# A two-layer decode kernel on one core: K in four interleaved DMAs for each pair of batches, `wo` in 4 KB runs, the stashed V returned later, and rstd applied after the projections

## The chip, the cores and the metric

The kernel runs on one core of one Trainium2 chip. The metric is device time in microseconds (us) of one execution. Ten of the 11 runs of before beside e5 lie within 0.5% of their median (185.98 us; 185.21 to 187.26). The profile is taken of one execution; its span, from the first to the last record, is some 2 us shorter than the device time.

## The reference

Four residual steps for 4 sequences of one token each: attention over a cache, a gated feed-forward block, and both again with the same weights. All arrays are bf16, D = 512, 32 query heads, 8 key heads, head size 128, F = 1792. The last W = 2048 positions of an 8192-long cache are used.

```python
def A(x, k_cache, v_cache, wq, wo):            # cut to what matters
    q = heads(x @ wq)                          # [4, 32, 1, 128]
    k = repeat(k_cache[:, :, Sk - W:, :], 4)   # W = 2048
    v = repeat(v_cache[:, :, Sk - W:, :], 4)
    p = softmax(q @ k.T * 128 ** -0.5)
    return merge(p @ v) @ wo

def B(x, w_gate, w_up, w_down):
    return (sigmoid(x @ w_gate) * (x @ w_up)) @ w_down

x = x + A(layernorm(x)); x = x + B(layernorm(x))
x = x + A(layernorm(x)); x = x + B(layernorm(x))
```

## The kernel before

K (16.8 MB) is loaded once and stays in SBUF for both attentions. V, `wq` and the feed-forward weights are streamed twice through a pool of 1 MB slots, `wo` is loaded once and kept. All DMAs but the 4 KB of x are issued by SyncE on one queue, in program order; each waits until a slot is free. A key head's 4 batches are two "pairs" of 1 MB: partition 2r + b holds row r (of 64) of batch b of the pair, and a row is 32 keys, 8 KB in one run.

```python
def pair_d(cache, h, bp):      # 64 rows x 2 batches, runs of 8 KB
    return cache[2 * bp:2 * bp + 2, h, SK - W:SK, :].rearrange("b (p j) d -> p b (j d)", p=64)

def load_k(h):
    where[("K", h)] = h
    for bp in range(2):
        dma("K%d_%d" % (h, bp), kpair(h, bp), pair_d(A_k, h, bp), w=tok(4 * h + 2 * bp), rate="bw_8k")

wo_d = A_wo.rearrange("(q p) n -> p q n", p=128)      # runs of 1 KB
def load_wo(hh):
    load(("wo", hh), 4, "bw_1k", (2 * SLOT, wo_d[:, hh * 2 * REP:(hh + 1) * 2 * REP, :], False))
```

One V pair survives the first attention as a "stash": VectorE transposes it into four PSUM banks and later back into a slot (the "unstash", line L502 of the kernel before).

```python
STASH = SB + PBS
def load_stash(name):
    ...
    def emit(s):
        for n, b in enumerate(STASH):
            dst = tile_ap(s)[:, n * 1024:(n + 1) * 1024].bitcast(F32)
            o = P.op("vector", "us%d" % n, c_dve(512), lambda v, dst=dst, b=b: v.transpose(dst, ps[:, b, :]), ...)
            ...
# order of loads after the first feed-forward weights:
load_wq(1)
load_stash(("V",) + keep[0] + (1,))
for h in range(HKV)[::-1]:
    ...
            if (h, bp) not in keep:
                load_v(h, bp, 1, 1)
```

The layer norm computes mean, variance and rstd before it writes the normalised `xn`. The query of a head is expanded to a block form by four copies on VectorE and ScalarE.

```python
def layer_norm(tag, b0, b1):
    # x*x; both sums; one f32 matmul with ones; mean; mean^2; var; Ln; Exp(-0.5 .); x - mean; times rstd -> xn
    ...
def q_unit(tag, h, k2):
    for a in range(4):
        dst = qbd[32 * a:32 * a + 32, ...]; src = qrep[32 * a:32 * a + 32, ...]
        ...                                           # VectorE for even a, ScalarE for odd a
```

The score matmuls read K after a transposition in place, so neighbouring keys of one batch lie two and two; per head there are 32 + 32 matmuls on V and 16 on `wo`.

```python
kt = kpair(hk, b // 2).rearrange("p (j c x i t) -> p c t i j x", c=2, x=16, i=2, t=2)
last = pe.matmul(ps[32 * gi:32 * gi + NR, bank, :], qbd[:, q0:q0 + NR],
                 kt[:, cp // 2, cp % 2, b % 2, :, :], start=(cp == 0), stop=(cp == 3))
```

## Time and profile before

| | before |
|---|---|
| device time, median of 3 runs | 186.11 us (185.71 to 186.42) |
| span of the profiled run | 184.4 us |
| DMA queue 1: bytes, share of 16 engines' span | 71.84 MB, 97.2% |
| first attention ends / second attention's first score matmul | 108.0 / 129.2 us |
| last V or `wo` matmul of the second attention | 172.3 us |
| last feed-forward activation `hT` written / last `w_down` landed | 179.5 / 181.75 us |

From the page of the kernel before: the span; the packets by size; the queue's bytes and its share of the 16 DMA engines' time; the chain of waits by engine.

```profile
span 184.4 us, 4421 instructions
...
DMA packets 15379, 72.12 MB, mean 391 GB/s; under 512 B 1144, under 2 KB 5248, under 8 KB 8704
...
q1 hardware_dynamic: 15352, 71.84, 97.2%
...
DMA 52%; PE 25%; SPq 16%; DVE 4%; issue 2%; ACT 0%
```

The engines have a packet in flight nearly all the time, so the time is near the sum of all packets' durations. That sum, over 16 engines, is 180.6 us by the packet records; an 8 KB packet takes 311 ns (median), 4 KB 159 ns, 2 KB 84 ns, 1 KB 48 ns, a semaphore write 9 ns.

The windows view of the kernel before. The columns are the stretch and its length, busy us (and instructions) of each engine, the granted TensorE clock as a share of full speed, the busy share of the DMA engines, and GB/s. Where the trace holds no record of the clock, the view prints 1.00; in before that is so until 24.6 us.

```profile
13.00:21.00 8.00, 1.86 (x44) 0.68 (x48) 6.87 (x11) 1.71 (x6) 0.00 (x0) 1.00 1.01 427
120.00:124.00 4.00, 1.73 (x20) 0.76 (x17) 1.25 (x8) 0.41 (x2) 0.00 (x0) 0.50 0.96 344
124.00:128.00 4.00, 1.43 (x28) 0.34 (x24) 3.14 (x6) 0.00 (x0) 0.00 (x0) 0.50 1.03 417
128.00:132.00 4.00, 3.97 (x52) 1.20 (x44) 1.90 (x7) 1.82 (x7) 0.00 (x0) 0.70 1.08 351
132.00:136.00 4.00, 3.50 (x50) 1.03 (x40) 3.08 (x12) 2.11 (x6) 0.76 (x4) 1.00 0.94 350
```

The first row is the K stream at 427 GB/s. I put the two rows at 350 GB/s down to V reloads that are issued late, since the first slot that comes free goes to the unstash.

The end of before in the timeline (start, length, engine, line, operation; in brackets the idle time before it and what ended it):

```profile
179.29 0.22 DVE L874 TENSOR_TENSOR hT<-ebuf,eg 128x56 bf16<-128x56 f32 x1
...
179.93 1.04 PE L905 MATMUL ps<-arena,hT 128*4 128x256 bf16 x16 [1.09 <-DMA arena<-in_B_w_down_dram]
...
181.17 1.01 PE L905 MATMUL ps<-arena,hT 128*4 128x256 bf16 x12 [0.20 <-DMA arena<-in_B_w_down_dram]
```

The last matmuls wait for the last weights. But `hT`, which PE's chain delivers, was ready at 179.5 us, only 0.4 us before the first of these weights (179.89 us).

### The profile page before, as it was taken

The page shows a single profiled execution, that of the slowest core. Times are in us where ns is not written, and L with a number is a line of the kernel's source. Part 1 is how long each engine was busy: PE and PEld are TensorE (multiplying, and loading weights), DVE is VectorE, ACT ScalarE, POOL GpSimd, SP SyncE. Part 2 cuts the span into 40 slices and gives each one's busy share as a digit, 9 for nine tenths or more (in the row PEclk, how much of TensorE's full clock was granted, in tenths as well). Part 3 has the DMA queues.
Part 4 walks back from the last instruction along what each step waited for, and adds up shares of the span by engine and source line. Part 5 has one row for each costly group of instructions (what it writes and reads, how often), then busy time and mean ns, then how long its engine had stood idle before and what let it go on. Part 6 is the DMA issues. An engine that isn't in the chain of part 4 may idle for free.

```text
span 184.4 us, 4421 instructions
## 1 busy us (share of the span) xinstructions
PE 101.2 (55%) x1944; PEld 54.7 (30%) x1944; DVE 89.5 (49%) x221; ACT 35.7 (19%) x100; POOL 14.8 (8%) x77
## 2 busy tenths in 40 slices
PE   0532423652807327173373545445979997994474
PEld 0101000332303323023232441210334653584422
DVE  5209998477592565925621531138463442340330
ACT  2003022240212103011020001001365442220010
POOL 4000000110000101010010000000022111120000
PEclk9999995585766756755555555555897897885569
DMA  5999999999999999999999999999999999999980
GB/s 198 425 427 427 425 403 391 411 421 419 409 387 425 419 421 403 392 419 419 400 391 414 412 407 393 403 350 417 330 396 419 419 423 416 418 416 402 412 341 24
DMA packets 15379, 72.12 MB, mean 391 GB/s; under 512 B 1144, under 2 KB 5248, under 8 KB 8704
## 3 DMA queue, kind: packets, MB, share of 16 engines
q1 hardware_dynamic: 15352, 71.84, 97.2%
q8 instruction: 15, 0.25, 0.5%
q14 instruction: 4, 0.03, 0.0%
q10 hardware_dynamic: 8, 0.00, 0.0%
HBM read 71.83 MB, written 0.00 MB: 390 GB/s over the span
## 4 chain that ended last, share of the span: by engine, by line
DMA 52%; PE 25%; SPq 16%; DVE 4%; issue 2%; ACT 0%
DMA arena<-in_A_v_cache_dram 33%; SPq L382 16%; PE ps L697 11%; DMA arena<-in_B_w_down_dram 9%; PE ps L770 8%; DMA arena<-in_A_wq_dram 5%; DMA arena<-in_B_w_up_dram 5%; PE ps L726 2%; PE ps L794 1%; DVE ps L492 1%; PE ps L626 1%; DVE nmax L705 1%; PE ps L749 1%; PE ps L905 1%; PE ps L852 1%
## 5 line engine op out<-in xcount | busy, mean ns | idle before, releaser
L770 PE MATMUL ps<-ebuf,arena 128*128 128x8 bf16 x1024 | 31.0, 167 | 29.7 <-DMA arena<-in_A_v_cache_dram 22.1
L697 PE MATMUL ps<-arena,qbd 128*16 128x512 bf16 x256 | 32.5, 626 | 16.9 <-DVE qbd L668 8.4
L770 PEld LDWEIGHTS ps<-ebuf,arena 128*128 128x128 bf16 x1024 | 28.8, 101 | 36.3 <-DMA arena<-in_A_v_cache_dram 32.5
L678 DVE STREAM_TRANSPOSE arena<-arena 128x1024 f32<-128x1024 f32 x32 | 37.9, 1219 | 3.3 <-DMA arena<-in_A_k_cache_dram 3.0
L705 DVE TENSOR_REDUCE nmax<-ps 128x1 f32<-128x512 f32 x16 | 11.0, 687 | 26.0 <-PE ps L697 26.0
L714 ACT ACTIVATE prow<-ps,nmax 128x512 bf16<-128x512 f32 x16 | 11.0, 687 | 39.6 <-DVE nmax L711 24.9
L671 ACT COPY qbd<-qrep 32x64 bf16<-32x64 bf16 x32 | 7.7, 241 | 40.9 <-PE ps L697 40.3
L697 PEld LDWEIGHTS ps<-arena,qbd 128*16 128x16 bf16 x256 | 6.1, 97 | 31.3 <-issue 22.0
L739 POOL CAST s<-psm 128x1 bf16<-128x1 f32 x16 | 3.0, 188 | 144.4 <-ACT prow L714 144.4
L778 DVE TENSOR_TENSOR onb<-ps,rinv 128x16 bf16<-128x16 f32 x16 | 2.9, 184 | 21.1 <-PE ps L770 21.1
L626 PE MATMUL ps<-arena,xn 128*4 128x512 bf16 x64 | 7.8, 582 | 7.6 <-DMA arena<-in_A_wq_dram 6.2
L794 PE MATMUL ps<-onb,arena 128*128 128x4 bf16 x256 | 9.1, 166 | 3.1 <-DVE onb L778 3.1
L731 ACT CAST prow<-ps 128x512 bf16<-128x512 f32 x16 | 9.4, 587 | 7.1 <-PE ps L726 7.0
L735 DVE STREAM_TRANSPOSE ebuf<-prow 128x256 f32<-128x256 f32 x16 | 7.0, 437 | 6.7 <-ACT prow L731 6.4
L852 PE MATMUL ps<-arena,xn 128*4 128x448 bf16 x64 | 6.5, 560 | 4.9 <-DVE xn L607 3.1
L794 PEld LDWEIGHTS ps<-onb,arena 128*128 128x128 bf16 x256 | 7.9, 101 | 4.1 <-DVE onb L778 2.8
L726 PE MATMUL ps<-prow,perm 64*128 64x256 bf16 x64 | 7.4, 315 | 2.4 <-ACT prow L714 2.3
L596 ACT ACTIVATE lnv<-lnv 128x4 f32<-128x4 f32 x4 | 0.8, 205 | 34.0 <-DVE lnv L593 34.0
L634 DVE STREAM_TRANSPOSE ebuf<-ps 128x512 f32<-128x512 f32 x4 | 2.9, 715 | 7.7 <-PE ps L626 7.6
L859 DVE STREAM_TRANSPOSE ebuf<-ps 128x448 f32<-128x448 f32 x4 | 2.6, 650 | 7.8 <-PE ps L852 7.8
L668 DVE COPY qbd<-qrep 32x64 bf16<-32x64 bf16 x32 | 5.3, 166 | 0.7 <-ACT qrep L657 0.2
L749 PE MATMUL ps<-sel_b,s 128*128 128x16 bf16 x48 | 3.8, 175 | 3.2 <-POOL s L743 2.4
(61 smaller groups left out, 68.1 us busy)
## 6 DMA issues: line engine op xcount, KB each, us to landing
arena<-in_A_v_cache_dram SPq DMA_DIRECT2D x30, 1024.0 KB, 16.8
arena<-in_A_k_cache_dram SPq DMA_DIRECT2D x16, 1024.0 KB, 16.0
arena<-in_A_wq_dram SPq DMA_DIRECT2D x8, 1024.0 KB, 9.4
arena<-in_A_wo_dram SPq DMA_DIRECT2D x4, 1024.0 KB, 24.3
arena<-in_B_w_gate_dram SPq DMA_DIRECT2D x4, 896.0 KB, 19.7
arena<-in_B_w_up_dram SPq DMA_DIRECT2D x4, 896.0 KB, 15.8
arena<-in_B_w_down_dram SPq DMA_DIRECT2D x2, 1024.0 KB, 12.5
arena<-in_B_w_down_dram SPq DMA_DIRECT2D x1, 768.0 KB, 7.0
```

Of the source, the lines that this page charges most:

```text
L382: o = P.op("sync", name, 0.0, lambda e, dst=dst, src=src: e.dma_start(dst, src), r=r, w=w, dma_bytes=nbytes, dma_rate=tm[rate])
L626: last = pe.matmul(ps[32 * hh:32 * hh + NB, qb, :], xn[:, c * NB:(c + 1) * NB], tile_ap(s)[:, o + hh * 512:o + (hh + 1) * 512], start=(c = ...
L671: P.op("scalar", "qe%s_%d" % (tag, a), c_act(64), lambda s_, dst=dst, src=src: s_.copy(dst, src), r=rd, w=[("q", k2, a)])
L678: P.op("vector", "T%d_%d" % (h, t), c_dve(1024), lambda v, v32=v32: v.transpose(v32, v32), r=[("slot", 4 * h + t)], w=[("slot", 4 * h + t)])
L697: last = pe.matmul(ps[32 * gi:32 * gi + NR, bank, :], qbd[:, q0:q0 + NR], kt[:, cp // 2, cp % 2, b % 2, :, :], start=(cp == 0), stop=(cp = ...
L705: lambda v: v.tensor_reduce(nmax[:, k2:k2 + 1], ps[:, bank, :], AXX, ALU.max),
L714: lambda a: a.activation(prow[:, :].rearrange("p (m x t) -> p m x t", x=16, t=2), ps[:, bank, :].rearrange("p (m t x) -> p m x t", x=16, t ...
L726: last = pe.matmul(ps[:, PBS[i], 0:256], perm[64 * i:64 * i + 64, jh * 128:(jh + 1) * 128], prow[64 * i:64 * i + 64, jh * 256:(jh + 1) * 2 ...
L731: lambda a: a.copy(prow[:, :].rearrange("p (y i t) -> p i y t", i=2, t=2), ps[:, PBS[0]:PBS[0] + 2, 0:256].rearrange("p i (y t) -> p i y t ...
L770: last = pe.matmul(ps[:, ob, bp * 8:bp * 8 + 8], src[:, j * 128:(j + 1) * 128], ev[:, j % 2, j % 16 // 2, x0:x0 + 8], start=(j == 0), stop ...
L794: last = pe.matmul(ps[:, WB, c * NB:(c + 1) * NB], tile_ap(s)[:, o + r_ * D + c * 128:o + r_ * D + (c + 1) * 128], ov[:, r_ * NB:(r_ + 1) ...
L852: last = pe.matmul(ps[32 * g:32 * g + NB, OBS[n], 0:NF], xn[:, c * NB:(c + 1) * NB], tile_ap(s)[:, o:o + NF], start=(c == 0), stop=(c == N ...
```

## The change

The intent has four parts. (1) `wo` comes in runs of 4 KB; for that, the rows of o must be permuted, by four more matmuls and one masked VectorE product for each head. (2) Four neighbouring keys of a batch shall lie side by side after the transposition, so that the score matmuls read longer runs: partition 8y + 4b + x holds key block 4y + x of batch b. Where one DMA wrote a pair, four DMAs now write 32 partitions each, every fourth partition. (3) The stashed V comes back behind two V reloads; with that, its four transpositions change their order, and the first scores of the second attention go to another PSUM bank, which VectorE clears first. (4) rstd no longer stands before `xn`: it multiplies the gate and q afterwards, q is expanded by matmuls, and the sigmoid ends in a reciprocal on VectorE.

```diff
-    wo_d = A_wo.rearrange("(q p) n -> p q n", p=128)
+    wo_d = A_wo.rearrange("(h p m) n -> p h (m n)", p=128, m=REP)
 ...
         def load_k(h):
             for bp in range(2):
-                dma("K%d_%d" % (h, bp), kpair(h, bp), pair_d(A_k, h, bp), w=tok(4 * h + 2 * bp), rate="bw_8k")
+                src = A_k[2 * bp:2 * bp + 2, h, SK - W:SK, :].rearrange("b (y x j) d -> x y b (j d)", y=16, x=4)
+                for x in range(4):
+                    dma("K%d_%d%d" % (h, bp, x), kpair(h, bp)[x:128:4], src[x], w=[("k", 4 * h + 2 * bp, x)], rate="bw_8k")
 ...
-                        kt = kpair(hk, b // 2).rearrange("p (j c x i t) -> p c t i j x", c=2, x=16, i=2, t=2)
+                        kt = kpair(hk, b // 2).rearrange("p (j c y i x t) -> p c t i j y x", c=2, y=4, i=2, x=4, t=2)
 ...
+                    last = pe.matmul(ps[:, ob, 144 + m * NR:144 + (m + 1) * NR], permo[:, m * 128:(m + 1) * 128], ov,
+                                     start=True, stop=True)          # 4 for each head, then a masked product
 ...
-        load_stash(("V",) + keep[0] + (1,))
+                    n_v += 1
+                    if n_v == 2:
+                        load_stash(("V",) + keep[0] + (1,))
 ...
     # layer norm: xn = x - mean at once; variance() is called after the first projection's matmuls
+                    P.op("vector", "gs%d" % k, c_dve(NH),
+                         lambda v: v.tensor_tensor(egv, tv, lnr[:, 0:nb].unsqueeze(1)..., ALU.mult), ...)
     # q_unit: four matmuls with eyew and one ScalarE copy in place of four copies of quarters
+                    last = pe.matmul(dst[:, :, :, a * REP:(a + 1) * REP], eyew[32 * hh:32 * hh + 32, 96 - 32 * a:224 - 32 * a],
+                                     src, start=True, stop=True)
```

## The prediction

> **What bounds the kernel now.** The DMA stream. The page shows 71.84 MB on queue 1, in flight for 97.2% of the 184.4 us span; the windows view shows 418 to 428 GB/s almost everywhere, PE busy 55%, DVE 49%. In the chain of waits DMA has 52%, PE 25%. From 128 to 165 us PE looks critical, but by 144 us the queue holds about 8 MB, and the last weights land at 181.1 us whatever PE does.
>
> **Cost of a packet,** median of the packet records: 8 KB 311 ns, 4 KB 159, 1 KB 48, a semaphore write 9. All packets at their medians on 16 engines give 174.3 us; data flows from about 2 to 179.5 us. So some 3 us are bubbles. The windows view shows the main ones: 119 to 122 us (205 GB/s at worst) and 128 to 136 us (351 and 350 GB/s). The second has a cause: four `wo` tiles and one V are resident, so four slots rotate. The unstash takes the first slot that the second q projection frees (124.1 us); the V reloads are issued only at 126.7, 129.2 and 131.7 us.
>
> **What the change does.**
> 1. `wo` in 4 KB runs: (64 x 48 - 16 x 159) ns = 0.53 us for each of four loads, **-2.1 us**, on the DMA stream, hence critical. Windows show about 349 GB/s for 3 us, four times. SP's stalls of 13 to 18 us, each on the V issue after a `wo`, should shrink; that gives no time.
> 2. K in four DMAs of 32 partitions: 48 more DMAs x 9 ns = **+0.4 us**. Runs stay 8 KB. An issue takes SP about 0.65 us, so K is issued at 403 GB/s; the 4 MB of `wq` ahead and V's 1 MB issues keep the queue filled. The score matmuls (1.91 us per 16 even at full clock, so bound by reading) read four neighbours: I expect 1.0 to 1.5 us. Off the critical path, except that K slots come free earlier near 130 us.
> 3. Stash behind two V reloads: these move to about 124 and 126.7 us. **-1.2 us** (about the loss at 128 to 136 us).
> 4. rstd off the way to xn: each layer norm about 1 us shorter (2.3 us from x to xn before), and q without per-quarter copies. The next weights mostly wait for DMA then: **-0.2 us**. The `o` permutation adds about 0.6 us per head, hidden, and undoes part of this before the first GLU.
>
> Sum -3.1 us: **183.0 us, range 180.8 to 185.2**. Faster by over 2% (below 182.4): 0.33; within 2%: 0.61; slower: 0.06.
>
> **What would show each step.** (1) No dip to 350 GB/s at `wo`, no 1 KB packets of it. (2) 8 KB packets still about 310 ns in the K stream, some 1900 packets under 512 B, score matmuls shorter. (3) First two V reloads issued before the third `wq` tile is used; 128 to 136 us above 400 GB/s. (4) First GLU matmul about 0.5 us sooner after the residual; DMA share unchanged. Span about 181.3.
>
> **What would make it wrong.** The K quarters. [...] K's 8 KB packets would take much longer than 310 ns; no DMA of before has this shape. 16.8 MB at half rate would cost tens of us. An issue above 0.65 us would starve the start. If the slow packets at 119 and 128 us are not a shallow queue, step 3 gives nothing: 184.2. If all bubbles go, 181.

The steps came to -2.1 + 0.4 - 1.2 - 0.2 = -3.1 us, hence 183.0 us. "Bound by reading" was an inference from a time that does not follow the clock (in before 1.93 us for 16 score matmuls at 0.50, from 91.62 us on, and 2.09 us at 1.00, from 131.39 us on); that the order of reading matters was measured later (1.10 and 1.16 us at 1.00 in after). The 1.0 to 1.5 us for 16 of them, the 0.2 us of step 4 and the 0.6 us per head are estimates.

## More of the kernel before

From the groups of the page of before (line, engine, operation, destination and source, count; busy us and mean ns; idle before it and what ended it): the score matmuls, and VectorE's transposition of K, which is the first user of K.

```profile
L697 PE MATMUL ps<-arena,qbd 128*16 128x512 bf16 x256 | 32.5, 626 | 16.9 <-DVE qbd L668 8.4
...
L678 DVE STREAM_TRANSPOSE arena<-arena 128x1024 f32<-128x1024 f32 x32 | 37.9, 1219 | 3.3 <-DMA arena<-in_A_k_cache_dram 3.0
```

## The result, and the profile after

| | before, same rounds | after |
|---|---|---|
| device time, median of 4 runs | 186.26 us (185.71 to 186.79) | 225.56 us (224.46 to 228.06) |
| ratio | | 1.21 (1.2034 to 1.2167) |
| span of the profiled run | 184.4 us | 224.1 us |
| all packets' time over 16 engines | 180.6 us | 210.6 us |
| last K landing | 88.2 us | 126.3 us |
| `hT` / last `w_down` landing | 179.5 / 181.75 us | 219.7 / 217.72 us |

A ratio is the mean time of a kernel's fast runs over the mean of the fast runs of before in the same rounds, so it is not quite the ratio of the medians quoted. One of the four runs of after, 228.06 us, is slow and is left out of it. Executions over 1.5% slower than the fastest of the same kernel are left out of the means. The kernel is 21% slower, far outside the range.

The same lines of the page of after:

```profile
span 224.1 us, 4627 instructions
...
DMA packets 13076, 72.13 MB, mean 322 GB/s; under 512 B 1912, under 2 KB 1920, under 8 KB 6400
...
q1 hardware_dynamic: 13048, 71.84, 93.4%
...
DMA 44%; SPq 23%; PE 23%; DVE 5%; issue 4%; ACT 1%; DVEq 0%; ACTq 0%
```

The bytes are the same, the 1 KB packets of `wo` are gone and 768 more semaphore writes are there, as intended. Yet the rate fell from 391 to 322 GB/s. The windows view of after:

```profile
13.00:21.00 8.00, 2.79 (x22) 1.38 (x22) 4.33 (x7) 1.13 (x4) 0.00 (x0) 1.00 1.02 279
120.00:124.00 4.00, 0.42 (x16) 0.33 (x13) 2.03 (x3) 0.00 (x0) 0.00 (x0) 1.00 1.02 361
124.00:128.00 4.00, 0.00 (x0) 0.00 (x0) 2.23 (x3) 0.00 (x0) 0.00 (x0) 1.00 1.01 396
128.00:132.00 4.00, 3.38 (x71) 1.94 (x72) 1.23 (x2) 0.00 (x0) 0.00 (x0) 1.00 0.62 227
132.00:136.00 4.00, 1.97 (x42) 1.28 (x39) 1.53 (x7) 1.37 (x3) 0.76 (x4) 1.00 0.93 353
136.00:140.00 4.00, 2.21 (x68) 2.04 (x68) 0.20 (x1) 0.00 (x0) 0.00 (x0) 1.00 0.73 248
```

The first row is the key: the K stream runs at 279 GB/s instead of 427, **at the same full DMA share** (1.02). The engines are not starved and none is unused; each packet takes longer. The packet records of 13 to 21 us say 473 ns for an 8 KB packet where before had 309. Before 169.2 us the trace of after holds no record of the clock, so the 1.00 in these rows says nothing. The share columns of 128 to 132 and 136 to 140 us (0.62 and 0.73) show a second loss: there the queue is empty, because K came so late that PE, which frees V's slots, is late as well.

```profile
L691 DVE STREAM_TRANSPOSE arena<-arena 128x1024 f32<-128x1024 f32 x32 | 38.5, 1226 | 21.9 <-DMA arena<-in_A_k_cache_dram 21.9
...
L710 PE MATMUL ps<-arena,qbd 128*16 128x512 bf16 x256 | 28.7, 593 | 30.6 <-DVE arena L691 30.1
```

These groups of the page of after show where the loss enters: VectorE waits 21.9 us for K (3.0 before), and the score matmuls wait 30.1 us for VectorE. The mean of a score matmul fell by only 5% (626 to 593 ns), but that mean mixes two clocks. After has its first clock record at 169.2 us: 1.00 for 6.8 us, then 0.50 until 220.4 us. Two rows of its windows view, and its score matmuls in the timeline:

```profile
172.00:176.00 4.00, 3.25 (x72) 1.99 (x65) 2.10 (x8) 2.79 (x8) 1.33 (x7) 1.00 0.99 403
...
180.00:184.00 4.00, 4.00 (x86) 2.18 (x82) 1.31 (x4) 1.42 (x4) 0.76 (x4) 0.50 1.02 422
```

```profile
169.46 1.10 PE L710 MATMUL ps<-arena,qbd 128*16 128x512 bf16 x16
...
171.25 1.16 PE L710 MATMUL ps<-arena,qbd 128*16 128x512 bf16 x16 [0.46 <-ACT qbd L684]
...
182.21 1.89 PE L710 MATMUL ps<-arena,qbd 128*16 128x512 bf16 x16
```

Where full clock is on record, 16 of them take 1.10 and 1.16 us (two heads); at 0.50 they take 1.88 to 1.89, and as much before the first record, where eight `wq` matmuls take 1.02 us, as in before at a recorded 0.50. Before itself needs 1.93 to 2.09 us for 16 at either clock, one interrupted head apart (at 1.00: the line at 131.39 us shown under e15). e8, which reads K in the order of after, repeats it (1.15 and 1.15 at 1.00, 1.88 at 0.50), and e1, which is after with K in the old order, behaves as before. So the new order did shorten the score matmuls by over 40% at the full clock, and by some 5% at half of it.

So two questions were open. Why are the packets of K slow? And what are the other three steps worth, under this loss?

### The profile page after: what moved, and what is told of

Same layout as the page of the kernel before. It is cut to its first block, busy times and chain, and to the rows that moved or that the text cites. A ratio compares the mean times of both kernels' runs of the same rounds, so it can differ in the third digit from the quotient of the medians.

```text
span 224.1 us, 4627 instructions
## 1 busy us (share of the span) xinstructions
PE 109.7 (49%) x2016; PEld 63.3 (28%) x2016; DVE 91.6 (41%) x209; ACT 31.2 (14%) x78; POOL 15.3 (7%) x79
## 4 chain that ended last, share of the span: by engine, by line
DMA 44%; SPq 23%; PE 23%; DVE 5%; issue 4%; ACT 1%; DVEq 0%; ACTq 0%
DMA arena<-in_A_v_cache_dram 27%; SPq L385 23%; DMA arena<-in_A_k_cache_dram 8%; PE ps L783 7%; PE ps L710 6%; DMA arena<-in_A_wq_dram 4%; DMA arena<-in_B_w_up_dram 4%; PE ps L884 2%; PE ps L739 2%; PE ps L822 2%; PE ps L643 1%; DVE ps L496 1%; DVE arena L691 1%; PE ps L942 1%; PE ps L679 1%
## 5 line engine op out<-in xcount | busy, mean ns | idle before, releaser
L783 PE MATMUL ps<-ebuf,arena 128*128 128x8 bf16 x1024 | 32.5, 168 | 49.5 <-DMA arena<-in_A_v_cache_dram 46.2
L691 DVE STREAM_TRANSPOSE arena<-arena 128x1024 f32<-128x1024 f32 x32 | 38.5, 1226 | 21.9 <-DMA arena<-in_A_k_cache_dram 21.9
L783 PEld LDWEIGHTS ps<-ebuf,arena 128*128 128x128 bf16 x1024 | 29.8, 104 | 56.7 <-DMA arena<-in_A_v_cache_dram 52.8
L710 PE MATMUL ps<-arena,qbd 128*16 128x512 bf16 x256 | 28.7, 593 | 30.6 <-DVE arena L691 30.1
L684 ACT CAST qbd<-ps 128x256 bf16<-128x256 f32 x16 | 5.9, 372 | 54.4 <-PE ps L710 48.1
L822 PE MATMUL ps<-onp,arena 128*128 128x16 bf16 x256 | 9.4, 174 | 1.5 <-DVE onp L806 1.0
L739 PE MATMUL ps<-prow,perm 64*128 64x256 bf16 x64 | 9.3, 388 | 0.7 <-ACT prow L727 0.7
L822 PEld LDWEIGHTS ps<-onp,arena 128*128 128x128 bf16 x256 | 8.1, 104 | 4.8 <-issue 3.1
L620 ACT ACTIVATE lnv<-ps 128x4 f32<-128x4 f32 x4 | 0.7, 174 | 51.5 <-PE ps L616 51.5
L679 PE MATMUL ps<-qh,eyew 32*128 32x64 bf16 x64 | 5.9, 224 | 2.8 <-ACT qbd L684 1.4
L806 DVE TENSOR_TENSOR onp<-ps,maskp 128x64 bf16<-128x64 f32 x16 | 3.5, 220 | 6.2 <-PE ps L801 6.1
```

The source lines that it names most:

```text
L679: last = pe.matmul(dst[:, :, :, a * REP:(a + 1) * REP], eyew[32 * hh:32 * hh + 32, 96 - 32 * a:224 - 32 * a], src, start=True, stop=True)
L691: P.op("vector", "T%d_%d" % (h, t), c_dve(1024), lambda v, v32=v32: v.transpose(v32, v32), r=[("k", 4 * h + t // 2 * 2, x) for x in range( ...
L739: last = pe.matmul(ps[:, PBS[i], 0:256], perm[64 * i:64 * i + 64, jh * 128:(jh + 1) * 128], prow[64 * i:64 * i + 64, jh * 256:(jh + 1) * 2 ...
L783: last = pe.matmul(ps[:, ob, bp * 8:bp * 8 + 8], src[:, j * 128:(j + 1) * 128], ev[:, j % 2, j % 16 // 2, x0:x0 + 8], start=(j == 0), stop ...
L822: last = pe.matmul(ps[:, WB, c * NR:(c + 1) * NR], tile_ap(s)[:, o + r_ * D + c * 128:o + r_ * D + (c + 1) * 128], ov[:, r_ * NR:(r_ + 1) ...
```

## The experiments

Sixteen kernels were run. A kernel with a single run is a single look; its time stands beside one or more runs of the kernel before on the same chip. Kernels that read wrong data are marked; the comparison with the reference passed them all, so that comparison says nothing about them (presumably the attention's share in the outputs is small; that was not measured).

### e1: after, with K loaded and read as before

```diff
-                for x in range(4):
-                    dma("K%d_%d%d" % (h, bp, x), kpair(h, bp)[x:128:4], src[x], w=[("k", 4 * h + 2 * bp, x)], rate="bw_8k")
+                dma("K%d_%d" % (h, bp), kpair(h, bp), pair_d(A_k, h, bp), w=[("k", 4 * h + 2 * bp, x) for x in range(4)], rate="bw_8k")
```

> The changed kernel with K loaded and read as before: one DMA of 128 partitions per pair, the old order in the score matmuls; wo runs, o permutation, stash and rstd stay changed. Theory (K quarters alone cost the 39 us): 8 KB packets back at a median of 310 ns, 71.84 MB at over 395 GB/s, about 182.5 us (ratio to before 0.97 to 0.99). Rival (something else of the change starves the queue between 128 and 152 us): those bubbles stay, at least 8 us, and the time is over 190 us.

Measured: 188.56 us (187.85 to 189.77), before 186.7; ratio 1.012 (1.0052 to 1.0188). The packets came back to 311 ns as expected, but neither text had the time right. The windows view of e1:

```profile
13.00:21.00 8.00, 3.20 (x26) 1.49 (x30) 6.74 (x9) 1.12 (x4) 0.00 (x0) 1.00 1.01 425
128.00:132.00 4.00, 4.00 (x43) 1.06 (x39) 3.16 (x6) 0.37 (x1) 0.00 (x0) 0.50 0.98 411
```

K alone costs about 37 us: the span goes from 224.1 to 186.7 us. The packet records split that: the packets' time over 16 engines falls from 210.6 to 177.3 us (33.3), the rest of the span, in which engines have no packet, from 13.5 to 9.4 us (4.1). And the other three steps together are not a gain of 3.5 us but a loss of about 2: their DMA time is 3.3 us less than before's, but the kernel ends later. So there are two causes to find.

### e8 and e7: is it the stride in HBM?

In the new layout each DMA reads 8 KB blocks that lie 32 KB apart. e8 is after with blocks that lie side by side; e7 is before with blocks 32 KB apart. Both read wrong keys. The theory is that the destination is to blame, every fourth partition; the mechanism given for it is cut here, as in the expectations of e3, e4, e5, e2 and e24, since no run shows one.

```diff
 e8 (against after)
-  ....rearrange("b (y x j) d -> x y b (j d)", y=16, x=4)
+  ....rearrange("b (x y j) d -> x y b (j d)", y=16, x=4)
 e7 (against before)
-  pair_d(A_k, h, bp)
+  A_k[2 * bp:2 * bp + 2, h, :, :].rearrange("b (p u j) d -> u p b (j d)", p=64, u=4)[0]
```

> The changed kernel, with the keys of each quarter of K taken from neighbouring 8 KB blocks (the 16 blocks of a quarter 8 KB apart instead of 32 KB). Wrong result on purpose: K's keys no longer match V's. Destination, sizes and number of DMAs as in the changed kernel. Theory (destination: [...]): 8 KB packets in the K stream stay near 474 ns, about 225 us. Rival (HBM source stride of 32 KB between engines): packets back at about 310 ns, below 190 us.

> The kernel before, K still in one DMA of 128 partitions, but its 64 blocks per batch taken 32 KB apart from the whole cache instead of 8 KB apart. Wrong result on purpose: other keys. Theory (destination): packets stay at 310 ns, 184 to 187 us. Rival (HBM source stride): 8 KB packets of K at 400 ns or more, over 200 us.

Measured: e8 226.96 us, K packets 466 ns (after: 473), 280 GB/s (279); e7 187.04 us, K packets 309 ns and 427 GB/s, both as in before. Whether the blocks lie 8 or 32 KB apart plays no part, in either layout.

### e3: four DMAs of 32 neighbouring partitions

```diff
-                dma("K%d_%d" % (h, bp), kpair(h, bp), pair_d(A_k, h, bp), ...)
+                for x in range(4):
+                    src = A_k[2 * bp:2 * bp + 2, h, SK - W:SK, :].rearrange("b (x p j) d -> x p b (j d)", x=4, p=16)[x]
+                    dma("K%d_%d%d" % (h, bp, x), kpair(h, bp)[32 * x:32 * x + 32], src, w=[("k", 4 * h + 2 * bp, x)], ...)
```

> The kernel before, same layout and right result, but each K pair loaded in four DMAs of 32 neighbouring partitions with neighbouring source blocks (40 DMA semaphores as in the change). Theory [...]: 8 KB packets in the K stream at 600 to 640 ns, about 235 us, slower than the changed kernel. Rival A (each DMA of two packets per engine pays a fixed cost): 474 ns as in the changed kernel, about 222 us. Rival B (HBM stride): 310 ns, about 187 us.

Measured: 242.05 us, K packets 596 ns, 222 GB/s, about half of before's 427. The theory's 600 to 640 ns is about twice before's 309 ns, and the agreement does not prove it: the source of each of these DMAs is 16 times 2 blocks, as in after, and that shape turns out to be slow by itself (e22: 252 GB/s). So what 32 neighbouring partitions cost was not shown, nor why after, whose DMAs reach every fourth partition, is slow.

### e5 and e4: is it the number of DMAs, or the number of partitions?

e5 splits a pair into four DMAs of all 128 partitions, 2 KB of each row. e4 splits it into two DMAs of 64 partitions, every second one, one batch each (right result).

```diff
 e5
+   src = ....rearrange("b (p x j) d -> x p b (j d)", p=64, x=4)[x];  dst = kpair(h, bp)[:, x * 1024:(x + 1) * 1024]
 e4
+   src = A_k[2 * bp + x, h, SK - W:SK, :].rearrange("(p j) d -> p (j d)", p=64);  dst = kpair(h, bp)[x:128:2]
```

> The kernel before, each K pair in four DMAs that each go to all 128 partitions (2 KB of every row), so as many and as large DMAs as in the change. Theory [...]: 2 KB packets of K stay at their 84 ns, K costs 0.2 us more per MB, 187 to 190 us. Rival (a fixed cost of some 340 ns per engine for each small DMA, which would also give 474 ns per 8 KB in the change): 2 KB packets at 115 to 130 ns, over 200 us.

> The kernel before, each K pair in two DMAs of 64 partitions in steps of two (one batch each, right result). Theory [...]: 8 KB packets in the K stream at 440 to 480 ns as in the change, about 220 us. Rival (a fixed cost per DMA): half as many DMAs, so about 390 ns, about 200 us.

Measured: e5 190.02 us; its 2 KB packets take 84 ns, the same as the other 2 KB packets of before, so it pays for the run length only and not for the count of DMAs. e4 185.91 us against 185.98 for before: 426 GB/s, 309 ns. The first form of my theory, that a DMA to a part of the partitions is slow by itself, fell here.

### e2 and e22: the shape of the source alone

Both keep before's layout and split a pair into four DMAs of 32 partitions, every fourth one: after's partitions, sizes and count. In e2 the source is a plain list of 32 blocks of one batch (right result). In e22 it is 16 times 2 blocks of one batch (wrong keys), the outer shape that after has. Theory A blames the 32 destination partitions, Theory B the 16 times 2 shape of the source.

```diff
 e2
+   src = A_k[2 * bp + x % 2, h, SK - W:SK, :].rearrange("(n u j) d -> u n (j d)", n=32, u=2)[x // 2]
 e22
+   src = A_k[2 * bp + x % 2, h, :, :].rearrange("(n v j) d -> v n (j d)", n=16, j=32)[0:2].rearrange("v n e -> n v e")
 both
+   dma("K%d_%d%d" % (h, bp, x), kpair(h, bp)[x:128:4], src, w=[("k", 4 * h + 2 * bp, x)], rate="bw_8k")
```

> The kernel before, same layout and right result, each K pair in four DMAs of 32 partitions in steps of four, as in the change, but each from one batch: the source is a list of 32 blocks, not 16 times 2. Theory A [...]: 8 KB packets of K near 474 ns, about 222 us. Theory B [...]: about 312 ns, 186 to 188 us.

> As the run before it in this call, but the source of each DMA is 16 times 2 blocks of one batch, from the whole cache: wrong result on purpose (other keys). Theory A: near 474 ns, as its partner. Theory B: near 474 ns, while its partner is at about 312 ns.

Measured: e2 185.50 us, e22 220.04 us, before 185.25 us. The K stream in the windows view, of e2:

```profile
13.00:21.00 8.00, 1.95 (x44) 0.76 (x48) 7.03 (x11) 1.71 (x6) 0.00 (x0) 1.00 1.02 426
```

and of e22:

```profile
13.00:21.00 8.00, 1.84 (x40) 0.62 (x40) 4.25 (x6) 1.71 (x6) 0.00 (x0) 1.00 1.02 252
```

The destination partitions, the bytes, the runs, the number of DMAs and the DMA share are the same; 309 ns became 521 ns for a packet and the kernel took 34.5 us longer. The cause is how the source is written as a shape. One more thing differs, the distance between the blocks (16 KB in e2, 128 KB in e22), but the DMAs of after and e8 are slow with 32 and 8 KB, and they differ from those of e2 otherwise only in taking two batches at once, as before does at full rate. DMAs of 32 partitions, as such, cost nothing measurable.

### e23 and e24: the same, with K in one DMA over 128 partitions

Before, with only the source's shape changed: 16 groups of 8 blocks, or 32 groups of 4 (both wrong keys). Nothing else differs from before; the transfer still covers all 128 partitions.

```diff
-   dma("K%d_%d" % (h, bp), kpair(h, bp), pair_d(A_k, h, bp), ...)
+   src = A_k[2 * bp, h, :, :].rearrange("(n v j) d -> n v (j d)", n=16, v=16)[:, 0:8]     # e23; e24: n=32, v=8, [:, 0:4]
+   dma("K%d_%d" % (h, bp), kpair(h, bp), src, ...)
```

> The kernel before, K still one 1 MB DMA over 128 partitions, but its source is 16 groups of 8 runs of 8 KB of one batch (wrong keys on purpose). If what costs is a source whose slowest dimension has exactly 16 entries, the 8 KB packets take 450 to 570 ns, the K stream runs at 250 to 290 GB/s at a full DMA share, and the time is 215 to 228 us. If the cost belongs to DMAs of 32 partitions, or to four DMAs in place of one, packets take 311 ns, 426 GB/s, 185 to 187 us.

> The same with 32 groups of 4 runs (wrong keys on purpose). My reading: [...] packets take 311 ns, 426 GB/s, 185 to 187 us. If any source of two outer dimensions that does not match the 64 rows of before were slow, 250 to 290 GB/s and over 210 us as in the other run.

Measured: e23 235.40 us, e24 187.49 us, before 186.23 us, one run each. The K stream of e23:

```profile
13.00:21.00 8.00, 1.83 (x40) 0.61 (x40) 4.25 (x6) 1.71 (x6) 0.00 (x0) 1.00 1.03 226
```

and of e24:

```profile
13.00:21.00 8.00, 1.89 (x44) 0.70 (x48) 6.90 (x11) 1.71 (x6) 0.00 (x0) 1.00 1.01 427
```

Slow and fast came out as expected, and e23 is slower than I had expected (592 ns for a packet where 450 to 570 was written, 235.4 us where 215 to 228 was). So a slowest dimension of exactly 16 in the source goes with the slow rate on 128 partitions too (226 GB/s); with 32 (e2, e24) or 64 (before, e4) it was 426 to 427 GB/s. Here the distance between the groups is a rival that was not run by itself: 128 KB in e23, 64 KB in e24. The number 16 was the only small one that was tried.

Why a source of 16 entries is slow was not shown: no record tells which engine moved which packet. The slow rates are not equal either: 222 GB/s in e3, 226 in e23, 252 in e22, 279 in after and 280 in e8.

### e13: is PE critical in the second attention?

The prediction said that the end is set by DMA, whatever PE does. The rival: PE is critical as well. e13 is before with 8 spare matmuls for each head of the second attention.

```diff
+            if tag.startswith("2."):
+                    for m in range(8):
+                        last = pe.matmul(ps[:, ob, 144 + m * NR:144 + (m + 1) * NR], ident_b[:, :], ov, start=True, stop=True)
```

> The kernel before, with eight spare matmuls per head in the second attention only (identity times the head's output, written where nobody reads). Theory (from 128 us on PE is as critical as DMA; the last weights come only 1 us before the last matmuls need them): about 0.3 us of PE per head, so +2 to +3 us (ratio 1.010 to 1.017). Rival (what the prediction said: the end is set by DMA whatever PE does): within 0.5 us of before.

Measured: 188.33 us (188.18 to 188.65), before 185.98; ratio 1.0119 (1.0084 to 1.0154). The end of e13 in the timeline:

```profile
182.62 0.22 DVE L881 TENSOR_TENSOR hT<-ebuf,eg 128x56 bf16<-128x56 f32 x1
...
182.98 1.75 PE L912 MATMUL ps<-arena,hT 128*4 128x256 bf16 x28 [0.40 <-DVE hT L881]
```

The last weights landed at 181.43 us, as before (181.75). The last matmuls now wait for `hT` and not for DMA. The words about the landing held; what I drew from them did not: the end is the later of two chains that lie within a microsecond of each other, so the spare matmuls, 2.9 us of PE's busy time in all (64 that overlap, in the groups of e13), are paid mostly in full. In the profiles `hT` comes 3.3 us later than in before and the end 2.5 us later, so before had about 0.8 us to spare.

### e14: `wo` in 4 KB runs, without the permutation of o

Before, with wrong results, since o's rows no longer fit.

```diff
-    wo_d = A_wo.rearrange("(q p) n -> p q n", p=128)
+    wo_d = A_wo.rearrange("(h p m) n -> p h (m n)", p=128, m=REP)
```

> The kernel before, with wo loaded in 4 KB runs and nothing else: o is not permuted, so the result is wrong on purpose. Theory (step 1 was sized right, and what it costs on PE is what eats it): every load behind comes 2.1 us earlier, the second attention starts that much earlier, 183.9 to 184.6 us, ratio 0.988 to 0.992. Rival (the gain is not on the critical path): ratio above 0.996.

Measured: 183.91 us (182.24 to 184.32), ratio 0.9866 (0.9828 to 0.9904), 2.5 us less. Its packets take 177.1 us where before's take 180.6. Step 1's DMA gain was sized about right, and it is worth its full size when PE gets no extra work: the first attention ends 1.7 us sooner (106.3 us), and the second 3.6 us sooner (168.7 for 172.3 us). The profiled run is the fastest of e14, 1.7 us under its median, so these two numbers flatter it.

### e17: e1 without step 1

e1 with `wo` as before and no permutation of o.

```diff
-    wo_d = A_wo.rearrange("(h p m) n -> p h (m n)", p=128, m=REP)
+    wo_d = A_wo.rearrange("(q p) n -> p q n", p=128)
-                    last = pe.matmul(ps[:, ob, 144 + m * NR:144 + (m + 1) * NR], permo[:, m * 128:(m + 1) * 128], ov, ...
```

> The changed kernel with K whole and in the old order, wo in 1 KB runs and no permutation of o; stash, rstd and the q expansion by matmuls stay. Theory: DMA loses the 2.1 us that wo gave, PE of the second attention is 0.12 to 0.25 us shorter per head than in the run with K whole; the two about cancel: 187.5 to 189.5 us. Rival (the o permutation is what cost the time in the run with K whole): below 186 us.

Measured: 187.20 us (186.93 to 188.52), ratio 1.0062 (1.0026 to 1.0097). Steps 3 and 4 alone, with no K quarters and no `wo`, still lose 1 us. Against e1 this run isolates step 1: e1 has the 2.5 us of e14 on its side and is still about 1.1 us slower (ratios 1.012 and 1.0062). So the permutation of o and what goes with it cost about 3.6 us, an estimate from three ratios whose intervals leave 2 to 5 us.

### e15: e17 with q expanded as before

Only the later stash and rstd's new place are left of the change.

```diff
-                    last = pe.matmul(dst[:, :, :, a * REP:(a + 1) * REP], eyew[...], src, start=True, stop=True)
+                if a % 2 == 0:
+                    P.op("vector", "qe%s_%d" % (tag, a), c_dve(64), lambda v, dst=dst, src=src: v.tensor_copy(dst, src), ...
```

> As the run without wo, but q expanded to its blocks as before, by copies on VectorE and ScalarE, not by matmuls for each head: what is left of the change is the later stash and rstd off the way to xn. Theory (the matmuls for q sit on a critical PE): 2 us or more under the run that has them, 184.5 to 186 us, a little under before (ratio 0.992 to 1.0). Rival (the stash or the rstd order is what costs): no faster than that run.

Measured: 187.02 us (186.53 to 188.25), ratio 1.0061 (1.0024 to 1.0097). I had expected at least 2 us under e17; there is no difference. That does not clear q's matmuls: in the second attention PE stands still twice in e15 for no reason that the profile names ("issue"), and once in before and in e17 (2.51 us).

```profile
168.17 0.27 PE L804 MATMUL ps<-onb,arena 128*128 128x4 bf16 x4 [1.90 <-issue]
...
174.61 0.28 PE L804 MATMUL ps<-onb,arena 128*128 128x4 bf16 x5 [2.44 <-issue]
```

And before:

```profile
168.41 1.77 PE L770 MATMUL ps<-ebuf,arena 128*128 128x8 bf16 x61 [2.43 <-issue]
```

In before and in after a packet of the instruction queue starts near the start of such a stall: at 166.05 us for a stall from 165.98 us in before, and at 207.35 for one from 207.85 us (2.17 us long) in after. The other 14 packets of that queue in before pass without a stall of PE of over 1 us that the profile puts down to "issue". Whether the packet is the cause was not tested.

The 1.8 us that e15 loses here beyond e17 in these profiles can hide a gain of nearly the expected size, so what q's matmuls cost stays open. What the later stash does is seen earlier in the timeline of e15:

```profile
128.33 2.51 DVE L502 STREAM_TRANSPOSE arena<-ps 128x512 f32<-128x512 f32 x4
...
128.44 2.04 PE L707 MATMUL ps<-arena,qbd 128*16 128x512 bf16 x16 [0.16 <-ACT qbd L681]
...
131.39 0.72 DVE L640 STREAM_TRANSPOSE ebuf<-ps 128x512 f32<-128x512 f32 x1 [0.55 <-PE ps L629]
132.03 0.65 DVE L715 TENSOR_REDUCE nmax<-ps 128x1 f32<-128x512 f32 x1
...
133.72 1.99 PE L707 MATMUL ps<-arena,qbd 128*16 128x512 bf16 x16 [0.39 <-DVE qbd L678]
```

And the same stage of before:

```profile
124.18 1.91 DVE L502 STREAM_TRANSPOSE arena<-ps 128x512 f32<-128x512 f32 x3 [1.34 <-PE ps L626]
...
129.15 2.01 PE L697 MATMUL ps<-arena,qbd 128*16 128x512 bf16 x16
...
131.22 0.69 DVE L705 TENSOR_REDUCE nmax<-ps 128x1 f32<-128x512 f32 x1 [1.84 <-PE ps L697]
131.39 2.09 PE L697 MATMUL ps<-arena,qbd 128*16 128x512 bf16 x16
```

In before the unstash (L502) mostly ran from 124 us, where VectorE and PE waited for `wq`. In e15 all 2.5 us of it stand on VectorE while the first head's scores are made. The maximum of these scores, which should start as they end (131.22 us in before, against an end of the scores at 131.2), starts at 132.03, 1.5 us after their end, and the second head's scores start at 133.72 instead of 131.39 us. The unstash itself is over at 130.84, 0.4 us after the scores; the rest of the delay is the transposition of the second q projection (L640), which now stands ahead of the maximum on VectorE and has to wait for PE. In before it comes behind the maximum. The DMA side did what was predicted: V's reloads were issued at 123.0 and 125.6 us (126.7 and 129.2 in before), and the last weights landed at 179.24 us, 2.5 us sooner. But `hT` came at 181.3 us, 1.8 us later, and here the second stall of PE (1.9 us more of stalls than in before) counts too. What the stash alone costs is measured by the next pair, whose profiles both have two such stalls.

### e18 and e19: the stash back in its old place

e18 is e15, and e19 is e1, with the stash restored early as in before (and with it the old PSUM bank and order of the transpositions, and no clearing).

```diff
+        load_stash(("V",) + keep[0] + (1,))
         for h in range(HKV)[::-1]:
 ...
-                    if n_v == 2:
-                        load_stash(("V",) + keep[0] + (1,))
```

> As the run with only the later stash and rstd, but the stash again ahead of the V reloads, with its first three transposes while PE waits for wq: what is left of the change is rstd off the way to xn. Theory (the four unstash transposes, 2.5 us of VectorE, land between the first two heads' score matmuls and their softmax): second attention ends about 1.5 to 2.5 us sooner, 184.5 to 185.7 us, ratio 0.990 to 0.998. Rival (the rstd order costs the time): 186.5 us or more.

> The changed kernel with K whole and in the old order, and the stash again ahead of the V reloads; wo runs, o permutation, q matmuls, rstd stay. Theory: the wo gain of 2.5 us is there for DMA, PE carries the permutation and the q matmuls, VectorE is free of the unstash: 1.5 to 2.5 us under the run with K whole, 186 to 187.2 us, about as before. Rival (the unstash costs nothing): as the run with K whole, about 188.5 us.

Measured: e18 185.44 us (184.64 to 186.63), ratio 0.9974 (0.993 to 1.0018); e19 186.55 us (186.0 to 186.9), ratio 1.0026 (0.999 to 1.0062). So the later stash costs about 1.6 us from e18 to e15, and 1.7 us from e19 to e1 (from the ratios to before, 0.0087 and 0.0094 apart, since the rounds and the chips were others). e18 is also step 4's layer norm by itself: about 0.5 us faster, not clear of the noise. Its profile has two of PE's stalls (2.07 and 2.17 us) where before has one, so it may be worth more; that was not tested. e19 is the whole change without the K quarters and the late stash. It has e14's packet time (177.1 us) and yet is not faster than before: from its first score matmul to the end of the second attention it takes 45.8 us, before 43.2 and e14 42.0. The difference to e14, 3.8 us over 8 heads (3.0 us by the ratios, as e14's profile is its fastest run), is 0.4 to 0.5 us for each head, and the work that e19 has and e14 has not is of that size: four permutation matmuls (4.2 us of PE over 16 heads, 0.26 us for each), four for q (5.3 us, 0.33 us for each), and a VectorE product between V's matmuls and those of `wo`. Of these only the permutation with its product was separated, by e1 and e17.

No valid kernel of these is clearly faster than before. The e14 gain needs the rows of o permuted by something that costs less than the gain. Before with `wo` in 4 KB runs, the permutation and the old q expansion would have been the next to try; it was not run.

## Why the prediction was right or wrong

The prediction, 183.0 us, was wrong by about 43 us, and the chance it gave to "slower" was 0.06.

**The step that failed.** It is step 2, "K in four DMAs of 32 partitions: 48 more DMAs x 9 ns = +0.4 us. Runs stay 8 KB." The sum took a packet's duration from its size. Runs did stay 8 KB, but such a packet took 473 ns in the K stream of after. Against e1 this costs 33.3 us of packet time and 4.1 us of emptier queue, 37 us in all. The prediction named the right suspect, the K quarters, and "tens of us", but gave it a small chance although "no DMA of before has this shape". The property that it named, DMAs of 32 partitions, was the wrong one: not the 32 partitions (e2 ran at 426 GB/s), but the source's 16 times 2 (e22 at 252, e2 at 426 GB/s; with 128 partitions 16 times 8 in e23 at 226, 32 times 4 in e24 at 427). Why such a source is slow was not shown, and the distance between the blocks of e23 and e24 differs too.

**The second mistake** was on the critical path: "From 128 to 165 us PE looks critical, but by 144 us the queue holds about 8 MB, and the last weights land at 181.1 us whatever PE does". They do land there (e13: 181.43 us), but `hT` was only 0.4 us ahead of the weights that it meets, and e13's 2.9 us of matmuls on PE cost 2.3 us of time. Two nearly equal chains were read as one bound and one slack.

**Step 1** was sized right for DMA ("-2.1 us"; e14 measured 2.5). "The `o` permutation adds about 0.6 us per head, hidden" was near in size and failed on "hidden": e1 against e17 puts it at about 3.6 us (an estimate, 2 to 5), some 0.45 us for each head of the second attention, where PE is critical, and the gain is gone (e19 against e14).

**Step 3** was right about its mechanism and wrong about its sign. The V reloads moved to 123.0 and 125.6 us ("about 124 and 126.7 us") and the stream ended sooner, but the 2.5 us of VectorE work, and the q transposition behind it, now stood before the first softmax: +1.6 us (e15 against e18) where -1.2 was expected.

**Step 4** was small, as said: "-0.2 us", measured about -0.5 for the layer norm and not clear of the noise (e18), with a second stall of PE in its profile that may hide more. Its other half, q by matmuls, stays unmeasured.

**The score matmuls** (16 of them "1.91 us") were expected at "1.0 to 1.5 us", and this part of step 2 held where the clock was full: 1.10 and 1.16 us. At half the clock they took 1.88 us, and in after nearly all of them ran so. Before had two keys of a batch side by side and took 1.93 to 2.09 us at either clock; after has four. So at the full clock four side by side were read faster than two; why was not shown. What the new order would bring with a fast load of K, no run shows. An estimate from the two kernels: 0.9 us for each head that gets the full clock (five of the eight in before's second attention), 0.1 us for the others.

## What to carry to other kernels

Size and count of a DMA's runs did not fix its rate here (e22 252 GB/s, e2 426): before relying on it, look at the outermost dimension of the source as it is written, and if it is exactly 16 with further rows under it (222 to 280 GB/s in five kernels here), try it with 32 or 64 (426 to 427 in e2, e24, e4 and before), or time one transfer of that shape by itself. The sign in this profile was a full DMA share with a low GB/s (1.02 and 279), which says that packets got slower (473 ns for 309) and not that the queue is short. Where the last matmul waits for DMA, ask how long its other operand had been ready: here it was 0.4 us, both chains were critical, and work taken from one and put on the other gained nothing. And before comparing a matmul's mean between two kernels, look at which stretches of each trace have a clock record, and compare at the same clock.
